# A weight clip that VectorE or GpSimd may take, ones columns on GpSimd, and new ranks for a planned schedule

## The chip, the cores and the metric

The kernel runs on one core of a Trainium2 chip. The metric is the device time of one execution in microseconds (us); lower is better. Three executions of the kernel before gave 1592.62, 1594.34 and 1591.09 us, median 1592.62. The engines are named as in the profile: PE (TensorE, matmul), PEld (its weight loads), DVE (VectorE), ACT (ScalarE), POOL (GpSimd), SP (SyncE, which here issues all DMAs).

## The reference

The input is q, k, v of 8 batches, 8 heads, 576 positions and 64 columns. First comes a linear attention, then two MLPs on its output of 4608 tokens by 512 columns:

```python
q_s = softmax(q, over the 64 columns);  k_s = softmax(k, over the 576 positions)
x = q_s @ (k_s^T @ v)                    # per batch and head
x = max(x @ w_in, 0)**2 @ w_out          # 512 -> 2048 -> 512
out = (sigmoid(x @ w_gate) * (x @ w_val)) @ w_out2   # 512 -> 1536 -> 512
```

The four MLP weights reach the kernel as 64-bit floats, seen as pairs of 32-bit words; q, k and v as 32-bit floats.

## The kernel before, in words

**Matmuls.** Tokens are taken in 9 blocks `j` of 512. Every float32 operand is split into a rounded part and the rest (`hi_of` on ACT, line 330; `lo_of` on DVE, line 333), and a product is three matmuls of 128x128 weights on 512 columns (`mm3`, lines 336 to 338). Blocks 0 and 1 and a part of block 2 go through the first layer with plain products, and block 0 through the second as well, up to about 216 us. From then on products run in a seven-product scheme over pairs of blocks (`plan_seven`), with sums of weights and of activations made by DVE.

**Weights.** 68 pieces of 128x512 are read (16 of `w_in`, 16 of `w_out`, 24 of `w_gate` and `w_val`, 12 of `w_out2`) and each is made from 64-bit to 32-bit floats by seven steps that `plan_raw` (line 456) lists: `wl` loads; `wa` (ACT, line 381) takes the magnitude of the high word, `wc` (ACT, line 387) scales the low word; `wp` (`w_clip`, DVE, line 391) clips the magnitude between two constants; `wb` (DVE, line 397) shifts and masks; `wg` (DVE, line 404) puts the sign in; `wr` (DVE, line 411) adds the low word. Then come the split (`wh` on ACT, `wo` on DVE, at line 425 the sums of weights `wm`), a store to DRAM, and fetches for later blocks.

**Attention.** `plan_k` (line 797) does k and v of a batch. `v_ones` (`vo`, lines 561 to 569) copies a column of ones ahead of each head's columns: on POOL for batch 0 (line 569), on ACT for batches 1 to 7 (line 567). `plan_q` (line 829) does the softmax of q for a block and a pair of heads. From block 2 on a row's 64 columns lie on two groups of partitions, so maxima and sums are exchanged between the groups: `q_swap` (`qaw`, `qbw`, line 700) is four POOL copies of 32x32. DVE waits for the exchange in `q_sub` (line 710) and in `q_sum` (line 729).

**What sets the order.** Every step is given to `Plan.add` with a rank (`key`), the engines that may do it with a price in us, what it comes after, and the buffers that it takes and gives back. `Plan.trace` (line 173) plays these prices through before the program is built: whenever an engine is free by the prices, it takes the step of lowest rank that is ready. That play emits the instructions, so it fixes each engine's order; on the chip each engine works through its own list in order, and waits where something is late. A step with two engines in its price table goes to whichever asks first; the engines are asked in the order DMA, PE, ACT, DVE, POOL. `SHIFT` (line 31) is a table of offsets that `add` puts on the ranks, by kind of step and, for some, by index; it alters nothing but ranks. Lists named `worder`, `fetched`, `xorder`, `sorder` keep loads, fetches and splits in a fixed sequence. In all that, only PE, ACT, DVE and POOL lists and the single DMA list of SP are affected by the ranks.

```python
add(t + 0.2, {DVE: 0.35}, ("wp",) + key, w_clip, key, after=[("wa",) + key])
add(t + 0.25, {DVE: 0.35}, ("wb",) + key, w_bits, key, after=[("wp",) + key])
```

Of the kernel before, what the change touches and what calls it, by code (L numbers as in the profile page):

```python
# [16 lines left out]
AF = mybir.ActivationFunctionType  # L17
ALU = mybir.AluOpType
AX = mybir.AxisListType

E_MIN = 2.0**-15
E_MAX = 2.0**17 - 2.0**-7
# [31 lines left out]
    "chi": {(): 66.5, (0, 14): 22.9, (0,): 50.9},  # L54
    "clo": {(): 169.7, (0, 0): 68.2, (0, 1): 96.7, (0, 8): -2.6, (0,): 104.5},
# [6 lines left out]
    "kdg": {(): -380.9},  # L62
    "kgm": {(): -139.8, (3, 0): 59.1, (3,): 37.6},
    "km": {(): 7.9, (0,): -1830.8, (1, 0): -54.8, (1, 1): 52.3, (1, 1, 0): 61, (3, 1): 16.6, (5, 1, 2): 6.5, (6, 0): 5.7, (6, 0, 0): 2.1,
        (6, 0, 3): 41.2, (6,): 12.8, (7, 0): 9.8, (7, 0, 0): -13.4, (7,): 4},
    "kp": {(): -972.4},
    "ks": {(): -453.2},
    "kt": {(): -32.2, (0, 0): -38.4, (0, 1): -34.1, (0,): -35.9, (1, 0): -75.3, (2, 0): -66, (7, 0): 5.4, (7,): 5.8},
    "kt2": {(): 17, (1, 0): -59, (4, 0): -3.7, (4,): 12.2, (5,): 84.3, (6,): 13.3, (7,): -12.4},
    "ost": {(1, 2): 10.4, (1, 3, 1): -18.6, (1,): -14.6, (2, 0): 20.2, (2, 1, 1): 8.2, (2, 3): 19.2, (2, 3, 1): -16.7, (2,): -1.8, (3, 2): 6.1,  # L70
# [190 lines left out]
def attention_mlp_mlp(  # L261
# [127 lines left out]
    def w_clip(key):  # L389
        t = wf[key]  # L390
        nc.vector.tensor_scalar(out=t, in0=t, scalar1=E_MIN, scalar2=E_MAX, op0=ALU.max, op1=ALU.min)
# [1289 lines left out]
```

## Time and profile before

| what | value |
|---|---|
| median of three executions | 1592.62 us |
| the profiled execution's own time | 1590.78 us |
| its span in the profile | 1589.0 us |
| PE busy | 1555.6 us, 98% |
| DVE busy | 1199.8 us, 76% |
| ACT busy | 941.3 us, 59% |
| POOL busy | 48.4 us, 3% |
| granted PE clock, whole span | 0.998 of full speed |

The profiled execution's own time is 1.8 us over its span and 1.8 us under the median of the three. Busy times are of the whole span; the stretches differ greatly, so the rows below go by stretch. A matmul's record runs on after the next has begun, so a small gap between two matmuls doesn't show as PE idle.

### The profile page before, as it was taken

The page shows a single profiled execution, that of the slowest core. Times are in us where ns is not written, and L with a number is a line of the kernel's source. Part 1 is how long each engine was busy: PE and PEld are TensorE (multiplying, and loading weights), DVE is VectorE, ACT ScalarE, POOL GpSimd, SP SyncE. Part 2 cuts the span into 40 slices and gives each one's busy share as a digit, 9 for nine tenths or more (in the row PEclk, how much of TensorE's full clock was granted, in tenths as well). Part 3 has the DMA queues.
Part 4 walks back from the last instruction along what each step waited for, and adds up shares of the span by engine and source line. Part 5 has one row for each costly group of instructions (what it writes and reads, how often), then busy time and mean ns, then how long its engine had stood idle before and what let it go on. Part 6 is the DMA issues. An engine that isn't in the chain of part 4 may idle for free.

```text
span 1589.0 us, 22941 instructions
## 1 busy us (share of the span) xinstructions
PE 1555.6 (98%) x7892; PEld 1280.7 (81%) x7892; DVE 1199.8 (76%) x2069; ACT 941.3 (59%) x1730; POOL 48.4 (3%) x122
## 2 busy tenths in 40 slices
PE   5899999999999999999999999999999999999998
PEld 3678878787888778888888888888888888888898
DVE  8999997899999999885957895348733682358446
ACT  7978765787686858675845563336433552345344
POOL 0011000010100020000000000000000000000000
PEclk9999999999999999999999999999999999999999
DMA  8896899999999889999897999657865667555996
GB/s 311 316 324 223 328 359 346 345 346 352 353 341 345 308 306 323 338 342 335 300 370 230 340 346 301 215 190 262 254 222 197 226 225 237 189 198 188 268 399 232
DMA packets 205619, 462.02 MB, mean 291 GB/s; under 512 B 78784, under 2 KB 78784, under 8 KB 205504
## 3 DMA queue, kind: packets, MB, share of 16 engines
q1 hardware_dynamic: 205504, 460.56, 83.3%
q8 instruction: 63, 1.03, 0.3%
q14 instruction: 52, 0.43, 0.1%
HBM read 364.54 MB, written 95.94 MB: 290 GB/s over the span
## 4 chain that ended last, share of the span: by engine, by line
PE 81%; DVE 11%; DMA 3%; ACT 2%; issue 2%; POOL 1%; SPq 0%; DVEq 0%; ACTq 0%; POOLq 0%
PE bank L336 27%; PE bank L338 26%; PE bank L337 26%; DVE whl L333 1%; DMA qt<-in_q_dram 1%; DVE qst L688 1%; POOL qsw L700 1%; PE kps L622 1%; DVE wf L404 1%; DVE wf L411 1%; DVE qt L711 1%; PE xps L771 1%; DVE g0hl L333 1%; DVE bS L333 1%; DVE wf L425 1%
## 5 line engine op out<-in xcount | busy, mean ns | idle before, releaser
L336 PE MATMUL bank<-bX,ws 128*128 128x512 f32 (+1 forms) x1176 | 441.6, 376 | 1.1 <-ACT bank L330 0.8
L338 PE MATMUL bank<-bX,ws 128*128 128x512 f32 (+1 forms) x1176 | 439.8, 374 | 0.0
L337 PE MATMUL bank<-bX,ws 128*128 128x512 f32 (+1 forms) x1176 | 439.8, 374 | 0.0
L336 PE MATMUL bank<-bS,ws 128*128 128x512 f32 (+1 forms) x868 | 331.4, 382 | 2.3 <-ACT x L330 1.4
L337 PE MATMUL bank<-bS,ws 128*128 128x512 f32 (+1 forms) x868 | 329.2, 379 | 0.0
L338 PE MATMUL bank<-bS,ws 128*128 128x512 f32 (+1 forms) x868 | 328.9, 379 | 0.0
L965 DVE TENSOR_TENSOR s<-s,bank 128x512 f32<-128x512 f32 (+1 forms) x171 | 108.8, 647 | 211.2 <-PE bank L338 180.7
L330 ACT ACTIVATE bS<-s 128x512 fp32r<-128x512 f32 (+1 forms) x330 | 192.8, 600 | 117.9 <-PE bank L338 89.8
L336 PEld LDWEIGHTS bank<-bX,ws 128*128 128x128 f32 x1176 | 221.5, 188 | 42.4 <-DVE s L963 1.2
L338 PEld LDWEIGHTS bank<-bX,ws 128*128 128x128 f32 x1176 | 221.5, 188 | 39.4
L337 PEld LDWEIGHTS bank<-bX,ws 128*128 128x128 f32 x1176 | 221.5, 188 | 39.1
L333 DVE TENSOR_TENSOR bS<-s,bS 128x512 fp32r<-128x512 f32 (+1 forms) x330 | 210.6, 653 | 35.5 <-ACT bS L330 35.1
L330 ACT ACTIVATE s<-bank 128x512 f32<-128x512 f32 (+1 forms) x227 | 128.6, 573 | 144.3 <-PE bank L338 142.6
L336 PEld LDWEIGHTS bank<-bS,ws 128*128 128x128 f32 x868 | 163.3, 188 | 36.2 <-issue 1.9
L338 PEld LDWEIGHTS bank<-bS,ws 128*128 128x128 f32 x868 | 163.3, 188 | 30.7
L337 PEld LDWEIGHTS bank<-bS,ws 128*128 128x128 f32 x868 | 163.4, 188 | 30.3 <-DVE bS L333 0.4
L892 DVE TENSOR_TENSOR s<-s,s 128x512 f32<-128x512 f32 (+1 forms) x192 | 120.4, 653 | 0.8
L330 ACT ACTIVATE bank<-bank 128x512 f32<-128x512 f32 (+1 forms) x108 | 59.1, 556 | 90.9 <-PE bank L338 82.0
L330 ACT ACTIVATE whl<-wf 128x512 fp32r<-128x512 f32 x127 | 78.7, 626 | 42.3 <-PE bank L338 14.7
L983 ACT ACTIVATE s<-s 128x512 f32<-128x512 f32 (+1 forms) x60 | 35.3, 588 | 91.7 <-DVE s L965 91.7
L333 DVE TENSOR_TENSOR whl<-wf,whl 128x512 fp32r<-128x512 f32 x127 | 86.1, 685 | 2.9 <-ACT whl L330 2.2
L700 POOL COPY qsw<-qst 32x32 f32<-32x32 f32 x112 | 45.9, 410 | 527.1 <-DVE qst L688 502.9
(116 smaller groups left out, 1846.3 us busy)
## 6 DMA issues: line engine op xcount, KB each, us to landing
ws<-w_out SPq DMA_DIRECT2D x217, 512.0 KB, 5.2
ws<-w_gv SPq DMA_DIRECT2D x210, 512.0 KB, 4.5
ws<-w_in SPq DMA_DIRECT2D x100, 512.0 KB, 6.2
w_out<-whl SPq DMA_DIRECT2D x49, 512.0 KB, 4.1
w_gv<-whl SPq DMA_DIRECT2D x42, 512.0 KB, 6.2
w_in<-whl SPq DMA_DIRECT2D x32, 512.0 KB, 5.8
kt<-in_k_dram SPq DMA_DIRECT2D x16, 640.0 KB, 5.7
x2r<-x SPq DMA_DIRECT2D x36, 256.0 KB, 5.1
```

Of the source, the lines that this page charges most:

```text
L330: nc.scalar.activation(out=dst, in_=src, func=AF.Copy)
L333: by_name[engine].tensor_tensor(out=dst, in0=src, in1=hi.bitcast(F32), op=ALU.subtract)
L336: nc.tensor.matmul(ps, ah, bh, start=first, stop=False, skip_group_check=True)
L337: nc.tensor.matmul(ps, ah, bl, start=False, stop=False, skip_group_check=True)
L338: nc.tensor.matmul(ps, al, bh, start=False, stop=last, skip_group_check=True)
L404: nc.vector.scalar_tensor_tensor(out=w, in0=high, scalar=-0x40000000, in1=w, op0=ALU.bitwise_and, op1=ALU.bitwise_or)
L411: by_name[engine].tensor_tensor(out=w, in0=w, in1=low, op=ALU.add)
L425: by_name[engine].tensor_tensor(out=t[0], in0=t[1], in1=t[2], op=op)
L700: nc.gpsimd.tensor_copy(out=other[32 * a:32 * a + 32], in_=st.rearrange("p g o -> p (g o)")[32 * b:32 * b + 32])
L892: by_name[engine].tensor_tensor(out=t[o], in0=t[a], in1=t[b], op=ALU.subtract)
L965: nc.vector.tensor_tensor(out=t, in0=t, in1=src, op=ALU.add)
L983: nc.scalar.activation(out=t, in_=t, func=AF.Sigmoid)
```

## The change

The clip `wp` may be done by POOL (priced 0.8) or by DVE (0.35); the columns of ones `vo` of all batches go to POOL, priced 0.35 in place of ACT's 0.22; the prices of the two exchanges go from 0.8 to 1.45; and the whole `SHIFT` table is another one, with more entries and wider values. All other prices, buffers and steps stay.

```diff
 SHIFT = {
-    "bcb": {(('G', 'c', 0, 0),): 22.1, (('G', 'c', 0, 2),): 199.4, (('G', 'c', 1, 0), 'T2'): 3.7, (('G', 0, 0, 0), 'T1'): -2.2,
...
-    "kdg": {(): -380.9},
...
-    "x": {(): -1764.4, (4, 2): 52.3},
+    "bcb": {(('G', 'c', 0, 2),): 180.67, (('G', 0, 0, 0),): -121.1, (('G', 0, 0, 2), 'T4'): -21.27, (('G', 0, 0, 2),): -8.01,
...
+    "kdg": {(): -1270.4},
...
+    "x": {(): -2931.32, (4, 2): 184.42, (6, 2): 54.47},
...
-    def w_clip(key):
+    def w_clip(key, engine):
         t = wf[key]
-        nc.vector.tensor_scalar(out=t, in0=t, scalar1=E_MIN, scalar2=E_MAX, op0=ALU.max, op1=ALU.min)
+        by_name[engine].tensor_scalar(out=t, in0=t, scalar1=E_MIN, scalar2=E_MAX, op0=ALU.max, op1=ALU.min)
...
-            add(t + 0.2, {DVE: 0.35}, ("wp",) + key, w_clip, key, after=[("wa",) + key])
+            add(t + 0.2, {POOL: 0.8, DVE: 0.35}, ("wp",) + key, w_clip, key, CHOSEN, after=[("wa",) + key])
...
-        if b:
-            nc.scalar.activation(out=pad[:, :, 1:2], in_=row[:, :, 2 * D:2 * D + 1], func=AF.Copy)
-        else:
-            nc.gpsimd.tensor_copy(out=pad[:, :, 1:2], in_=row[:, :, 2 * D:2 * D + 1])
+        nc.gpsimd.tensor_copy(out=pad[:, :, 1:2], in_=row[:, :, 2 * D:2 * D + 1])
...
-            add(key + 2.5 * step, {ACT: 0.22}, ("vo",) + x, v_ones, *x, after=[("kt",) + n if b else ("vt",) + x])
+            add(key + 2.5 * step, {POOL: 0.35}, ("vo",) + x, v_ones, *x, after=[("kt",) + n if b else ("vt",) + x])
...
-            add(key + 0.3 * step, {POOL: 0.8}, ("qaw",) + n, q_swap, j, p, after=[("qa",) + n], take=["qw"])
+            add(key + 0.3 * step, {POOL: 1.45}, ("qaw",) + n, q_swap, j, p, after=[("qa",) + n], take=["qw"])
...
-            add(key + 2.3 * step, {POOL: 0.8}, ("qbw",) + n, q_swap, j, p, after=[("qb",) + n], take=["qw"])
+            add(key + 2.3 * step, {POOL: 1.45}, ("qbw",) + n, q_swap, j, p, after=[("qb",) + n], take=["qw"])
```

## Rows read from the trace of the kernel before

**Rows 1.** The stretches of the span: length, busy time of each engine, clock, DMA.

```profile
core 0: us, PE busy (x) PEld busy (x) DVE busy (x) ACT busy (x) POOL busy (x), PEclk, DMA share, GB/s
0.00:40.00 40.00, 22.39 (x154) 14.29 (x155) 34.45 (x66) 30.12 (x77) 2.49 (x10) 0.91 0.87 309
40.00:80.00 40.00, 34.78 (x239) 24.74 (x240) 37.92 (x73) 37.48 (x70) 0.00 (x0) 1.00 0.90 319
80.00:120.00 40.00, 38.15 (x257) 29.18 (x256) 36.35 (x65) 30.51 (x56) 7.76 (x24) 1.00 0.96 324
120.00:200.00 80.00, 80.00 (x400) 65.44 (x400) 78.03 (x136) 61.10 (x107) 8.46 (x25) 1.00 0.76 276
200.00:240.00 40.00, 37.48 (x163) 30.03 (x162) 36.99 (x63) 27.72 (x50) 0.00 (x0) 1.00 0.93 351
240.00:600.00 360.00, 358.88 (x1995) 287.38 (x1994) 335.26 (x572) 261.24 (x485) 29.67 (x64) 1.00 0.94 338
600.00:1589.00 989.00, 983.90 (x4693) 829.60 (x4691) 640.81 (x1100) 493.12 (x890) 0.00 (x0) 1.00 0.79 269
```

**Rows 2.** PE in order of time: start, duration, what; idle before it and releaser.

```profile
30.00 0.50 PE L336 MATMUL bank<-x,whl 128*128 128x512 f32 x1 [1.07 <-ACT x L330]
...
216.31 0.50 PE L336 MATMUL bank<-bS,ws 128*128 128x512 f32 x1 [1.41 <-ACT x L330]
...
218.18 0.50 PE L336 MATMUL bank<-bS,ws 128*128 128x512 f32 x1 [0.90 <-DVE x L1092]
```

**Rows 3.** The chain that ended last, 200 to 220 us: start, us, what.

```profile
200.11 0.34 DVE wf L391
...
203.32 0.35 DVE wf L391
...
217.52 0.61 DVE x L1092
218.13 0.04 issue
218.18 0.50 PE bank L336
```

**Rows 4.** The clips of line 391 by stretch: length, DVE busy (count), clock, DMA.

```profile
0.00:40.00 40.00, 2.10 (x5) 0.91 0.87 309
40.00:120.00 80.00, 5.98 (x15) 1.00 0.93 322
120.00:217.00 97.00, 4.90 (x12) 1.00 0.79 291
```

**Rows 5.** Groups of instructions on POOL: busy us, mean ns, idle before.

```profile
L700 POOL COPY qsw<-qst 32x32 f32<-32x32 f32 x112 | 45.9, 410 | 527.1 <-DVE qst L688 502.9 <-DVE kri L630 15.9 <-DVE qst L710 4.2
L569 POOL COPY vt<-vt 128x5 f32<-128x5 f32 x4 | 1.8, 463 | 10.5 <-DMA vt<-in_v_dram 10.5
masks.py:199 POOL TENSOR_SCALAR_AFFINE_SELECT ident<-ident 128x128 f32<-128x128 f32 x1 | 0.3, 292 | 0.1
```

**Rows 6.** POOL in order of time.

```profile
10.88 0.19 POOL L569 COPY vt<-vt 128x5 f32<-128x5 f32 x1 [9.58 <-DMA vt<-in_v_dram]
86.75 0.93 POOL L700 COPY qsw<-qst 32x32 f32<-32x32 f32 x4 [73.19 <-DVE qst L688]
561.60 5.21 POOL L700 COPY qsw<-qst 32x32 f32<-32x32 f32 x4 [14.17 <-DVE qst L688]
```

**Rows 7.** DVE in order of time beside that last exchange.

```profile
564.12 0.69 DVE L333 TENSOR_TENSOR bS<-p,bS 128x512 fp32r<-128x512 f32 x1
564.72 0.69 DVE L411 CUSTOM_DVE_ANT_0 wf<-wraw,wf 128x1024 uint16<-128x1024 uint16 x1
565.32 0.69 DVE L333 TENSOR_TENSOR bS<-p,bS 128x512 fp32r<-128x512 f32 x1
566.84 0.19 DVE L710 TENSOR_TENSOR qst<-qst,qsw 128x32 f32<-128x32 f32 x1 [0.83 <-POOL qsw L700]
```

**Rows 8.** Who waited for the exchanges: us in total, times, longest us.

```profile
DVE qst L710 <- POOL qsw L700: 3.4, 5, 0.8
DVE qst L729 <- POOL qsw L700: 3.4, 5, 0.8
```

**Rows 9.** The ones of line 567 by stretch: length, ACT busy (count), clock, DMA.

```profile
0.00:40.00 40.00, 0.31 (x2) 0.91 0.87 309
40.00:120.00 80.00, 0.92 (x6) 1.00 0.93 322
120.00:217.00 97.00, 0.70 (x4) 1.00 0.79 291
```

More of the change, by code (lines that the diff above doesn't have):

```diff
@@ L31 @@
 SHIFT = {
[22 rows of a table removed]
-    "chi": {(): 66.5, (0, 14): 22.9, (0,): 50.9},
-    "clo": {(): 169.7, (0, 0): 68.2, (0, 1): 96.7, (0, 8): -2.6, (0,): 104.5},
[6 rows of a table removed]
-    "kdg": {(): -380.9},
[L63 to L68, printed above, removed]
@@ L69 @@
-    "kt2": {(): 17, (1, 0): -59, (4, 0): -3.7, (4,): 12.2, (5,): 84.3, (6,): 13.3, (7,): -12.4},
-    "ost": {(1, 2): 10.4, (1, 3, 1): -18.6, (1,): -14.6, (2, 0): 20.2, (2, 1, 1): 8.2, (2, 3): 19.2, (2, 3, 1): -16.7, (2,): -1.8, (3, 2): 6.1,
[25 rows of a table removed]
-        ('out', 2, 2): 137.9, ('out', 2, 3): -149.4, ('out', 3): 89.3, ('out',): 45.2, ('out2', 1, 2): -24.1, ('out2', 2, 2): 22.5, (): 151.6},
[9 rows of a table removed]
-        ('out', 0, 0): 53.8, ('out', 0, 2): 51.1, ('out', 1, 1): 51.8, ('out2', 0): 40.3, (): 100.8},
[8 rows of a table removed]
-        ('out', 0, 'S4'): -33.9, ('out', 2): -65.1, ('out',): 96.9, (): 18.5},
[19 rows of a table removed]
[43 rows of a table added]
@@ new lines @@
+    "chi": {(): 3.71, (0, 12): 7.02, (0,): 53.98},
+    "clo": {(): 471.13, (0, 0): 264.69, (0, 1): 252.23, (0,): 409.28},
[7 rows of a table added]
+    "kdg": {(): -1270.4},
+    "kgm": {(): -899},
+    "km": {(): -21.94, (0,): -3197.62, (1,): 179.2, (5, 0, 0): -170.86, (5, 0, 2): 19.14, (5,): 32.04, (6, 1): -33.99, (6, 1, 2): -31.67,
+        (6, 1, 3): -35.07, (6,): 4.07, (7,): -34.37},
+    "kp": {(): -1463.85},
+    "kr": {(): 154.16, (6, 1): -165.66, (6,): -34.79, (7, 0): -127.02, (7, 1): -190.16},
+    "ks": {(): -1599.48},
@@ new lines @@
+    "kt": {(): -105.72, (0, 0): 53.12, (0, 1): 54.99, (0,): -146.43, (3, 1): 10.54, (5, 0): -5.58, (5, 1): -28.28, (5,): -9.82, (6, 0): -43.56,
+        (7, 0): 3.27, (7, 1): -24.77},
+    "kt2": {(): 21.69, (1, 1): 222.61, (4, 0): -86.63, (5, 0): -61.14, (5,): 78.64, (6, 0): -23.55, (6, 1): -24.1, (7,): -12.87},
+    "ost": {(): -13.3, (0,): -53.34, (1, 0): -65.18, (1, 0, 0): -44.46, (1, 1): -61.21, (1, 2): -55.1, (1, 2, 0): 131.94, (1, 3, 1): -112.12,
[18 rows of a table added]
+        ('out', 1): -266.74, ('out', 1, 1): -168.29, ('out', 1, 2): -73.67, ('out', 1, 3): -70.86, ('out', 2): -385.76, ('out', 2, 0): -10.82,
+        ('out', 2, 3): -313.06, ('out', 3): -93.35, ('out',): 90.34, ('out2', 0, 0): -9.25, (): 680.79},
[4 rows of a table added]
+        ('in',): 269.94, ('out', 0): 25.98, ('out', 1): -233.29, ('out', 1, 3): -87.44, ('out',): 146.19, ('out2', 2): -21.27, ('out2', 2, 2): -98.53,
+        (): 173.94},
@@ new lines @@
+    "wc": {('gv', 1, 3): -32.27, ('gv', 3): -42.2, ('gv', 4, 0): 32.32, ('gv', 4, 1): -166.53, ('gv', 4, 3): -165.23, ('gv', 5, 0): -142.99,
+        ('in',): 2663.43, ('out', 0): 49.57, ('out', 0, 2): -67.87, ('out', 1, 1): -136.8, ('out', 2): -385.57, ('out', 2, 3): -295.23,
+        ('out',): 14.89, (): 743.55},
[33 rows of a table added]
+        ('in', 2, 3): 40.69, ('out', 0, 1): -93.29, ('out', 0, 2): -53.83, ('out', 1): -166.73, ('out', 2): -318.93, ('out', 3): -43.47,
[16 rows of a table added]
+        ('out', 3, 3): -210, (): 108.56},
[4 rows of a table added]
+        ('in', 3, 1): -149.83, ('in',): -20.09, ('out', 0): -19.43, ('out', 0, 3): -142.5, ('out', 0, 7): -90.34, ('out', 1): -132.45,
+        ('out', 2): -49.7, ('out', 2, 3): -34.56, ('out', 3): -85.29, ('out', 3, 3): -82.99, ('out', 3, 4): -90.87, ('out', 3, 5): -121.43,
[9 rows of a table added]
```

219 rows, old and new, of the table SHIFT are left out of this document.

## The prediction

> **What bounds the kernel now.** I read the stretches first [rows 1]. The PE clock is at its upper level, 2.4 GHz, in every stretch but the first 40 us, so the clock has nothing to give. What counts is PE's idle time, length minus busy: 17.6 us in 0 to 40, 5.2 in 40 to 80, 1.9 in 80 to 120, none in 120 to 200, 2.5 in 200 to 240, 1.1 in 240 to 600, and 5.1 from 600 to the end. The change alters no matmul, so only this idle time can be won. The last 5.1 us are the results' way out after the last matmul. The first 17.6 us come almost all before the first large matmul at 30.00 us [rows 2], while k and q are loaded and go through the softmax. That leaves 5.2 + 1.9 + 2.5 + 1.1 = 10.7 us within reach, nearly all of it before 240 us.
>
> Who holds PE up there? DVE is busy 37.92 of 40 us and ACT 37.48 of 40 in the stretch 40 to 80, and DVE 78.03 of 80 in 120 to 200 [rows 1]. The chain of waits runs through DVE up to 218 us, the clips of line 391 among its pieces, and it passes to PE's matmuls at 218.18, where PE had sat idle for 0.90 us on a DVE copy, after 1.41 us on an ACT split a little before [rows 2, 3]. After that PE has its matmuls fed: DVE still has 335 of 360 us of work up to 600, yet PE idles only 1.1 us. So DVE's load up to 217 us is the thing to watch, and what the change does to DVE later is worth at most that 1.1 us.
>
> **The change part by part.**
>
> The clip. Of the 68 clips 5 + 15 + 12 = 32 lie before 217 us [rows 4]; 27 of them after 40 us. On the chain one clip occupies 0.34 to 0.35 us of DVE [rows 3]. The plan asks DVE first, but a DVE that is busy over nine tenths of the time is rarely free at the moment when a clip becomes ready, so nearly all 27 should go to POOL. Taken off: 27 x 0.35 = 9.5 us of DVE.
>
> What it costs on POOL, no row shows for this shape. The nearest rows are the columns copy of 128x5 in 0.19 us [rows 6] and the select of 128x128 in 0.292 us [rows 5]: (0.292 - 0.19) / 123 columns is 0.83 ns a column, and 512 columns would take 0.19 + 507 x 0.00083 = 0.61 us, an estimate. 27 of these are 16.5 us, and POOL is busy only 16.2 us between 80 and 200 [rows 1]: POOL has room. The clip is one link of a chain on one piece (magnitude, clip, shift, sign, add), so 0.61 in place of 0.35 us delays only that piece, which the plan fetches ahead.
>
> What it pays back is DVE waiting for POOL. The exchange shows how POOL fares beside a busy DVE. Undisturbed, four copies take 0.93 us; beside a row of back-to-back DVE instructions they took 5.21 us, and DVE's own instructions of 128x512 kept their 0.60 us pace and 0.69 us length meanwhile [rows 6, 7]. So DVE isn't slowed by POOL's small copies; it pays where it needs the result: 0.83 us of idle time at 566.84 [rows 7]. Over the 28 exchanges (112 copies of four each [rows 5]) that happened 10 times and cost 3.4 + 3.4 = 6.8 us [rows 8], 0.24 us an exchange. The clip's cost to DVE lies between nothing (it fits behind other DVE work) and that 0.83 us each time. I take the mean of the exchange, the nearest row with the same pair of engines: 27 x 0.24 = 6.5 us. Net relief of DVE: 9.5 - 6.5 = 3.0 us. Ends: 9.5 us won, or 27 x (0.83 - 0.35) = 13 us lost.
>
> Here a page speaks against the change. Between POOL and DVE the rows show POOL waiting and DVE not. The Trainium skill, "SBUF — State Buffer", section "Who interferes with whom", says that the two share one pair of ports as an exclusive lock: a POOL instruction that starts first keeps it for its whole length, and a DVE instruction with two SBUF inputs is fully blocked until then. No row here has a POOL instruction long enough to show it; by that rule the clip would be no relief but a loss, and it stands among the rivals.
>
> The price of the exchanges. Nothing new runs; DVE's waiting step is placed 0.65 us later, so that other ready work goes in front of it. 12 of the 28 exchanges lie before 200 us (24 + 25 copies, by the counts in [rows 1]), and 12 x 0.24 = 2.9 us of DVE waiting is the most to win. I take half, 1.5 us; at the other end nothing.
>
> The columns of ones. 28 ACT copies become POOL copies. Before 217 us these are 2 + 6 + 4 = 12, with 0.31 + 0.92 + 0.70 = 1.9 us of ACT [rows 9]. ACT is the fuller engine only between 40 and 80 us; I take 0.5 us of PE time, between 0 and 1.9. On POOL such a copy takes 0.19 us by itself and 0.463 on average [rows 5, 6], and it is now queued with clips and exchanges; k's matmuls wait for it, four steps later in the chain, so I cost it at nothing. If it came behind a starved clip it could cost its k block what the longest exchange lost, 4.3 us.
>
> The ranks. They change the order on every engine and on SP's list of DMAs, not the work. They could win the rest of the 10.7 us, or undo some of the stretch after 600 us where PE now runs without a gap. Nothing in the trace says which; I take 0. No list gets a DMA more or less.
>
> **The sum.** 3.0 + 1.5 + 0.5 = 5.0 us off the span of 1589.0, thus 1584.0, and 1585.8 for the profiled execution's own 1590.78. The median of the runs is 1.8 us above that execution, so the forecast is 1587.6 us, 0.3% faster. Its own range goes from the whole 10.7 us won (1581.9) to the bound of what can be told from no change, 0.2% or about 3.2 us (1589.4).
>
> **The rivals.**
>
> *No measurable change*, 1592.6, within 3.2 us: what DVE wins comes out in 120 to 200 us, where PE is busy 40 of 40 anyway, or is paid back in waits of just 0.35 us a clip, the point where gain and loss meet. For it: PE's busy share is 98% and most of the DVE-heavy stretch shows no PE idle at all. Against it: the chain ran through DVE up to 218 us. That most clips stay on DVE, since DVE is asked first, also ends here.
>
> *DVE waits for POOL* (slower): the plan sets the shift step 0.95 us after the clip begins, but beside back-to-back DVE work POOL gets no turn until DVE stops at that very step, as at 566.84. If that decides 60% of the 27 clips at 0.83 us and the rest cost nothing, DVE loses 16 x 0.83 - 27 x 0.35 = 3.8 us; if it decides nearly all, 13. I take 8: 1600.4 us. It decides from a mean wait of 0.35 us a clip. For it: one third of the exchanges ended in such a wait. Against it: the mean was 0.24.
>
> *POOL holds DVE up* (slower): a running clip makes the next DVE instruction stand for the estimated 0.61 us. 27 x (0.61 - 0.35) = 7.0 us, 1599.6 us. Against it: no DVE instruction beside the exchanges is longer than its fellows [rows 7]. For it: those copies have 32 columns. This is what the page's rule above makes of it.
>
> *Faster by more than the sum*: the new order also brings forward the first large matmul, out of the 17.6 us of the first stretch. Three us more would be 1579.
>
> **How the numbers follow.** Forecast and the better end: 0.50 faster. No measurable change: 0.24. Slower: 0.14 for DVE waiting and 0.12 for POOL holding, 0.26 together. The range goes down to 1579, the best case, and up to 1603, past both slower rivals and short of the 13 us bound (1605.6), which leaves out some 1 in 10.
>
> **What would show it.** Right: line 391 appears on POOL over 50 times at about 0.6 us or more, DVE's busy time falls by some 20 us over the span, PE idle between 40 and 240 us falls from 9.6 to about 5 us, and after 600 us PE has its 5.1 us of idle time and no more. Wrong on the clip: waits of DVE's line 397 on POOL of over 9.5 us before 217 us (the first slower rival), or DVE instructions of 128x512 lasting 1.2 us and more beside POOL clips (the second). Wrong on the ranks: PE idle times on DMA or ACT where there were none, above all after 240 us, or a first large matmul well away from 30 us.

## The result: 1.2% slower, and the profile after

The changed kernel takes 1611.38 us (median of four runs, 1609.54 to 1615.25) against 1592.62: a ratio of 1.0121, interval 1.0098 to 1.0143. Its profiled execution took 1609.54 us with a span of 1607.7, so 18.7 us more than the span before. The line numbers have moved: 391 of before, the clip, is 446; 397, the shift, is 452; 404, the sign, is 459; the matmuls of lines 336 to 338 are now 391 to 393, and the splits of 330 and 333 are 385 and 388.

Here are the stretches of the changed kernel, as in [rows 1].

```profile
core 0: us, PE busy (x) PEld busy (x) DVE busy (x) ACT busy (x) POOL busy (x), PEclk, DMA share, GB/s
0.00:40.00 40.00, 21.49 (x142) 14.20 (x143) 31.56 (x57) 28.23 (x71) 15.93 (x18) 0.87 0.79 292
40.00:80.00 40.00, 33.23 (x229) 23.55 (x228) 36.33 (x62) 35.62 (x64) 15.33 (x9) 0.96 0.87 306
80.00:120.00 40.00, 37.27 (x207) 28.59 (x206) 34.22 (x58) 27.75 (x48) 13.62 (x24) 1.00 0.87 298
120.00:200.00 80.00, 77.59 (x422) 61.55 (x421) 71.56 (x119) 57.12 (x100) 35.59 (x45) 0.98 0.74 263
200.00:240.00 40.00, 38.44 (x165) 30.25 (x164) 36.76 (x61) 26.52 (x47) 7.08 (x3) 1.00 0.88 312
240.00:600.00 360.00, 357.27 (x1977) 286.42 (x1976) 328.07 (x551) 260.45 (x470) 80.07 (x86) 1.00 0.95 341
600.00:1607.70 1007.70, 999.68 (x4761) 839.09 (x4759) 653.51 (x1110) 505.22 (x909) 23.32 (x20) 1.00 0.81 268
```

DVE is *less* busy than before in every stretch up to 600 us (71.56 of 80 against 78.03 in 120 to 200), and yet PE stands idle more: 18.5 + 6.8 + 2.7 + 2.4 + 1.6 + 2.7 + 8.0 = 42.7 us against 33.4. Idle time is only half of the loss, though: for the same 7892 matmuls PE's busy time grew as well, from 1555.6 to 1565.0 us; the last section comes back to that. A less busy DVE on the path that feeds PE doesn't mean relief; here it means that DVE itself waits. The groups on POOL, as in [rows 5], and the waits for them, as in [rows 8], say for what:

```profile
L446 POOL TENSOR_SCALAR wf<-wf 128x512 f32<-128x512 f32 x54 | 119.4, 2216 | 425.0 <-ACT wf L436 406.3 <-DMA w_in<-whl 8.3 <-DVE qst L740 5.6
L752 POOL COPY qsw<-qst 32x32 f32<-32x32 f32 x112 | 45.5, 406 | 134.7 <-DVE qst L740 129.3 <-DVE qst L781 1.3 <-DVE kri L682 0.4
L621 POOL COPY vt<-vt 128x5 f32<-128x5 f32 x32 | 25.5, 827 | 166.9 <-DMA vt<-in_v_dram 101.8 <-PE bank L393 64.9
```

```profile
DVE wf L452 <- POOL wf L446: 25.8, 23, 2.5
```

54 of the 68 clips went to POOL, and there a clip takes long. The view of line 446 gives the shortest and the median in ns, on POOL and on DVE:

```profile
L446 POOL TENSOR_SCALAR wf<-wf x54: 1914/1956/5270, 16.5 to 916.1; 128x512 f32<-128x512 f32 x54
L446 DVE TENSOR_SCALAR wf<-wf x14: 420/427/431, 73.8 to 910.7; 128x512 f32<-128x512 f32 x14
```

At best 1.914 us, where the plan says 0.8, my estimate said 0.61, and DVE needs 0.42. So in 23 places DVE came to the shift of a piece before POOL had clipped it, and stood still for 25.8 us in all.

The second loss shows in DVE's own durations. This is DVE in order of time, and below it POOL:

```profile
56.80 0.68 DVE L466 CUSTOM_DVE_ANT_0 wf<-wraw,wf 128x1024 uint16<-128x1024 uint16 x1
57.40 1.10 DVE L459 SCALAR_TENSOR_TENSOR wf<-wraw,wf 128x512 int32<-128x512 int32 x1
58.42 0.41 DVE L631 TENSOR_TENSOR kmx<-kt 128x256 f32<-128x256 f32 x1
59.29 0.43 DVE L452 TENSOR_SCALAR wf<-wf 128x512 int32<-128x512 int32 x1 [0.46 <-POOL wf L446]
```

```profile
56.83 2.43 POOL L446 TENSOR_SCALAR wf<-wf 128x512 f32<-128x512 f32 x1 [4.53 <-ACT wf L436]
```

The clip begins at 56.83, and the sign step at 57.40 takes 1.10 us, where its median is 0.685; then the shift at 59.29 waits 0.46 us for the clip's end. Both losses meet in this one clip; over the span they do so in 8 clips. The sign step's shortest, median and longest durations, first before and then after:

```profile
L404 DVE SCALAR_TENSOR_TENSOR wf<-wraw,wf x68: 628/685/697, 18.2 to 898.5; 128x512 int32<-128x512 int32 x68
```

```profile
L459 DVE SCALAR_TENSOR_TENSOR wf<-wraw,wf x68: 629/685/1111, 18.9 to 922.2; 128x512 int32<-128x512 int32 x68
```

Counted over all DVE instructions: 33 last over 60 ns longer than the median of their form (same line, tiles and shape), the first at 19.82 us and the last at 916.23; every one overlaps a clip on POOL; none is over by more than 0.426 us; the sum is 11.8 us. In the kernel before there is none. So a clip holds DVE up, but mostly for some 0.41 us and not for its whole 1.92. "Held up" below always is this count (the expectations say 11.2 us, and 12.9 for c2, by a slightly different one).

### The profile page after: what moved, and what is told of

Read it like the earlier page. It is cut to its first block, busy times and chain, and to the rows that moved or that the text cites. A ratio compares the mean times of both kernels' runs of the same rounds, so it can differ in the third digit from the quotient of the medians.

```text
span 1607.7 us, 22980 instructions
## 1 busy us (share of the span) xinstructions
PE 1565.0 (97%) x7892; PEld 1283.6 (80%) x7892; DVE 1192.0 (74%) x2012; ACT 940.9 (59%) x1705; POOL 190.9 (12%) x204
## 4 chain that ended last, share of the span: by engine, by line
PE 69%; DVE 14%; DMA 4%; issue 4%; POOL 3%; ACT 3%; SPq 1%; DVEq 0%; POOLq 0%; ACTq 0%
PE bank L391 23%; PE bank L392 23%; PE bank L393 23%; POOL wf L446 3%; DVE bS L388 2%; DVE s L944 1%; DVE whl L388 1%; DVE wf L459 1%; DMA vt<-in_v_dram 1%; DVE wf L466 1%; DMA wraw<-in_moe_w_out_dram 1%; DVE qst L740 1%; SPq L424 1%; DVE bX L388 1%; POOL qsw L752 1%
## 5 line engine op out<-in xcount | busy, mean ns | idle before, releaser
L446 POOL TENSOR_SCALAR wf<-wf 128x512 f32<-128x512 f32 x54 | 119.4, 2216 | 425.0 <-ACT wf L436 406.3
```

The source lines that it names most:

```text
L446: by_name[engine].tensor_scalar(out=t, in0=t, scalar1=E_MIN, scalar2=E_MAX, op0=ALU.max, op1=ALU.min)
```

## The experiments

Two theories came first: **C**, the clip on POOL is the loss; **R**, the new ranks are. In the plan both hang together, since a price alters the order. So some runs keep the plan as it is and alter only which engine an instruction is issued on, in the same place of the order.

**Same order, clips back on DVE (a1)**

```diff
-        by_name[engine].tensor_scalar(out=t, in0=t, scalar1=E_MIN, scalar2=E_MAX, op0=ALU.max, op1=ALU.min)
+        nc.vector.tensor_scalar(out=t, in0=t, scalar1=E_MIN, scalar2=E_MAX, op0=ALU.max, op1=ALU.min)
```

> The changed kernel with every step in the same place and the same ranks, but the clips that it gave to POOL are issued on DVE at that place of the order. Theory C (the clip on POOL is the loss: 1.92 us where 0.8 was planned, DVE waiting 25.8 us for it and held up for 11.2 us): back to about the kernel before, 1587 to 1597 us, although DVE gets some 19 us of clips more. Theory R (the new ranks are the loss): stays at 1604 us or more.

1597.62 us, ratio to before 1.0024 (1.0014 to 1.0034), 0.6 us above the range of theory C. Although DVE has 54 clips more to do, 13.8 of the 18.8 us are gone by the medians (some 11 to 19 by the two intervals). Theory C holds for these. What is left, 4.7 us over the kernel before (2.2 to 5.4 by the interval), is not the clip on POOL.

**The kernel before, same order, clips on POOL (d1)**

```diff
-        nc.vector.tensor_scalar(out=t, in0=t, scalar1=E_MIN, scalar2=E_MAX, op0=ALU.max, op1=ALU.min)
+        nc.gpsimd.tensor_scalar(out=t, in0=t, scalar1=E_MIN, scalar2=E_MAX, op0=ALU.max, op1=ALU.min)
```

> The kernel before, same ranks, prices and order, with all 68 clips issued on POOL. Theory C: in this order the shift step stands close behind the clip, so DVE waits for POOL on most pieces, over 1 us each, and the time is well above the change's, 1612 to 1660 us. Theory R: 1590 to 1600 us.

1633.66 us, 1.0252 (1.0237 to 1.0267): 40.3 us lost with the old ranks untouched, with all 68 clips on POOL. In this order the shift stands close behind the clip, and the wait grows:

```profile
DVE wf L397 <- POOL wf L391: 65.0, 45, 5.6
```

**Is it the clip's length? (b4)** The clip with its lower bound alone:

```diff
-... scalar1=E_MIN, scalar2=E_MAX, op0=ALU.max, op1=ALU.min)
+... scalar1=E_MIN, scalar2=None, op0=ALU.max)
```

> The changed kernel with the clip cut to its lower bound (one operation in place of two; the upper bound is left out). If POOL's time is spent on the operations, the clip falls from 1.92 to 1.0 to 1.4 us while it still reads 512 columns and holds DVE for about 0.41 us. Theory L (the length of the clip in its chain is the loss): 1598 to 1606 us. Theory H (holding up DVE is the loss): 1608 to 1613 us, as the change. If the clip stays at 1.9 us this tells nothing between them.

```profile
L446 POOL TENSOR_SCALAR wf<-wf x54: 1482/1614/4829, 17.3 to 910.1; 128x512 f32<-128x512 f32 x54
```

```profile
DVE wf L452 <- POOL wf L446: 17.3, 18, 1.8
```

The operations were not most of the clip's time: it fell to 1.48 us at best, not to 1.0 to 1.4. That was enough: DVE's waiting fell by 8.5 us, it was held up much as before (11.4 us), and the time fell by 6.6 us to 1604.76 (1.0070, 1.0055 to 1.0085). The length counts through DVE's waits.

**Is it the holding up? (c2, e2)** Clips on DVE; wherever POOL had a clip, two instructions of 256 columns that nobody waits for:

```diff
+    spare_o = cst.tile([128, 256], mybir.dt.uint8, name="spare_o")
...
-        by_name[engine].tensor_scalar(out=t, in0=t, scalar1=E_MIN, scalar2=E_MAX, op0=ALU.max, op1=ALU.min)
+        nc.vector.tensor_scalar(out=t, in0=t, scalar1=E_MIN, scalar2=E_MAX, op0=ALU.max, op1=ALU.min)
+        if engine == POOL:
+            for _ in range(2):
+                nc.gpsimd.tensor_scalar(
+                    out=spare_o.rearrange("p (o c) -> p o c", c=128), in0=ident.rearrange("p (o c) -> p o c", o=1).to_broadcast([128, 2, 128]),
+                    scalar1=E_MIN, scalar2=E_MAX, op0=ALU.max, op1=ALU.min,
+                )
```

> As a1 (the changed kernel's order, clips on DVE), but wherever the change gave a clip to POOL, POOL does two instructions of 256 columns on a constant tile that nobody waits for. They hold DVE for some 0.2 us each and keep POOL busy, but are no link of a weight's chain. Theory H: 1604 to 1612 us. Theory L: 1596 to 1601 us, as a1. In between, the parts can be read off: a1 is 1597.6.

```profile
L450 POOL TENSOR_SCALAR spare_o<-ident x108: 1052/1116/4866, 13.8 to 631.4; 128x256 uint8<-128x256 f32 x108
```

1610.02 us, 1.0104 (1.0089 to 1.0119), 12.4 us above the same kernel without them (a1). No piece of weight waits for them; DVE is held up for 13.5 us (74 instructions, at most 0.23 us each). But k's matmuls need ones that now stand behind such an instruction in POOL's list, so it was run again with the ones of batches 1 to 7 on ACT:

```diff
-        nc.gpsimd.tensor_copy(out=pad[:, :, 1:2], in_=row[:, :, 2 * D:2 * D + 1])
+        if b:
+            nc.scalar.activation(out=pad[:, :, 1:2], in_=row[:, :, 2 * D:2 * D + 1], func=AF.Copy)
+        else:
+            nc.gpsimd.tensor_copy(out=pad[:, :, 1:2], in_=row[:, :, 2 * D:2 * D + 1])
```

> As c2 (clips on DVE, two idle POOL instructions of 256 columns where the change had a clip), with the ones of batches 1 to 7 on ACT, so that nothing but the exchanges stands behind them. Theory H (holding up DVE, 12.9 us in c2): 1606 to 1611 us, near c2's 1610. Theory Q (c2 lost its 12.4 us to the ones behind the idle instructions): 1598 to 1602 us.

1607.34 us, 1.0083 (1.0068 to 1.0098), with 13.1 us of holding up. The same kernel without the idle work is c3 below, 1598.52 us, so the loss is still 8.8 us. POOL work that nobody needs thus costs 8.8 to 12.4 us for some 13 us of holding up; some 3 us may be due to what stands behind it, but the intervals of the two runs overlap.

**The ones (e1, c3, d2).** The same edit in the changed kernel, clips on POOL, then in the kernel with clips on DVE; and the reverse, all ones on POOL, in the kernel before at the same order:

> The changed kernel, clips on POOL, with the columns of ones of batches 1 to 7 issued on ACT at the same place of the order. Theory Q (part of the loss is k's matmuls waiting for ones that stand behind clips in POOL's list, 6.7 us of waits of the weight loads on line 446): 1602 to 1607 us. Theory D (the loss is DVE's time alone: 25.8 us waiting, 11.2 us held up): 1608 to 1613 us.

> As a1, with the columns of ones of batches 1 to 7 issued on ACT at the same place of the order. Theory O (the remaining 4.7 us over before come from ones on POOL, that take 1.16 us on average there): 1590 to 1594 us. Theory R (they come from the ranks): 1596 to 1600 us.

> The kernel before, same ranks, prices and order, with the ones of batches 1 to 7 issued on POOL. All theories: within 3 us of before, 1590 to 1596 us, since no POOL work of any length stands in front of them.

1612.77 us (1.0114, 1.0097 to 1.0132) beside the change's 1.0121; 1598.52 us (1.0027, 1.0014 to 1.0039) beside 1.0024; 1593.47 us (0.9996, 0.9987 to 1.0005) beside before. All three show no difference: where the ones of batches 1 to 7 are made is worth nothing that can be told. I had laid 6.7 us at their door: waits of PE's weight loads that the profile puts down to a clip on POOL. 2.3 of them went without effect. The other one, 4.4 us (4.7 in the first of these runs), is no wait for ones. It stands before the first batch's matmuls, whose ones were ready at 13.17 us. In the changed kernel these rows lead up to the matmuls:

```profile
12.97 0.20 POOL L621 COPY vt<-vt 128x5 f32<-128x5 f32 x1 [0.23 <-DMA vt<-in_v_dram]
21.44 0.43 DVE L452 TENSOR_SCALAR wf<-wf 128x512 int32<-128x512 int32 x1 [0.80 <-POOL wf L446]
21.78 1.48 DVE L658 TENSOR_TENSOR kt<-kt,bank 128x1280 f32<-128x1280 f32 x1
23.29 1.27 ACT L662 ACTIVATE kt<-kt 128x1280 f32<-128x1280 f32 x1 [0.81 <-DVE kt L658]
24.66 2.43 PE L674 MATMUL bank<-vt,kt 128*64 128x65 f32 x40 [4.14 <-POOL wf L446]
```

PE began 0.1 us after ACT's exponential of k (line 662), which had waited for DVE's subtraction (line 658), and that stood behind a shift that waited for a clip. So the clip reaches PE here through DVE's list, not through the ones. PE's wait is not all new: in the kernel before it idles 3.06 us ahead of the same matmuls.

**The prices and the ranks (a3, a4, b2, c4).** The changed kernel with the clip on POOL priced at what it takes:

```diff
-            add(t + 0.2, {POOL: 0.8, DVE: 0.35}, ("wp",) + key, w_clip, key, CHOSEN, after=[("wa",) + key])
+            add(t + 0.2, {POOL: 1.95, DVE: 0.35}, ("wp",) + key, w_clip, key, CHOSEN, after=[("wa",) + key])
```

> The changed kernel with the clip on POOL priced at 1.95 us in the plan, all else the same. Theory C by its part that the plan was wrong on the length: the waits of DVE's line 452 on POOL fall from 25.8 us to under 10, the time to 1596 to 1604 us; DVE is still held up by about 0.4 us a clip. Theory R: about 1608 to 1614 us, since the ranks are the same.

```profile
DVE wf L452 <- POOL wf L446: 3.3, 5, 1.9
40.00:80.00 40.00, 29.66 (x209) 20.58 (x210) 32.26 (x57) 31.43 (x56) 10.90 (x7) 0.96 0.88 314
```

1608.44 us, 1.0100 (1.0079 to 1.0120). The waits went, as expected, and the time hardly moved: theory C's range failed, and the time lies in the one given for theory R. PE's idle time in 40 to 80 us is now 10.3 us (29.66 busy) where the change has 6.8. A new price made a new order (48 clips on POOL in place of 54), with ranks that were not made for it. That this order is what it lost to is argued, not shown. How much a price can do by itself, the next three show: the old ranks with all the new prices; the same with the clip on DVE alone; and the kernel before with nothing but the exchange at 1.45.

```diff
-            add(key + 0.3 * step, {POOL: 0.8}, ("qaw",) + n, q_swap, j, p, after=[("qa",) + n], take=["qw"])
+            add(key + 0.3 * step, {POOL: 1.45}, ("qaw",) + n, q_swap, j, p, after=[("qa",) + n], take=["qw"])
...
-            add(key + 2.3 * step, {POOL: 0.8}, ("qbw",) + n, q_swap, j, p, after=[("qb",) + n], take=["qw"])
+            add(key + 2.3 * step, {POOL: 1.45}, ("qbw",) + n, q_swap, j, p, after=[("qb",) + n], take=["qw"])
```

> The clip, the ones and the exchange prices as changed, with the ranks of the kernel before. Theory C: slower than before by about as much as the change or more, 1602 to 1618 us. Theory R: 1588 to 1597 us.

> The ranks of before, the clip on DVE alone; of the change only the ones on POOL and the longer exchange prices. Theories C and R both: within 5 us of before, 1588 to 1597 us. Theory O (columns of ones that queue behind other POOL work cost k's matmuls time): 1598 us or more.

> The kernel before with the price of the two exchanges at 1.45 in the plan and nothing else changed. Theory P (ranks fit only the prices that they were made for, so any new price upsets the order): 1600 to 1630 us, a good part of the 32 us that old ranks with the new prices of ones and exchanges lost. If a truer price helps by itself: 1585 to 1593 us.

1644.36 us (1.0319, 1.0302 to 1.0335), 1625.58 (1.0205, 1.0187 to 1.0223) and 1627.93 (1.0210, 1.0195 to 1.0225). The first lies above the range of either theory, the second above that of theories C and R both. The last is the kernel before with two numbers in the plan changed and the same instructions on every engine, and it loses 34 us. The first two differ in the plan by the clip alone, and by 18.8 us; but their orders differ too, so this is no price of the clip. I had blamed the ones for whatever the second would lose; the exchange's price alone loses as much. In the last one, DVE waits only 1.7 us for the exchanges, and new PE idle time has come: 11.6 us in 240 to 600, where the kernel before has 1.1, and 9.0 us in two stretches that hold no exchange at all and in which it has none. First the two stretches in the kernel before, then in this run:

```profile
760.00:800.00 40.00, 40.00 (x177) 32.91 (x177) 39.57 (x67) 33.05 (x60) 0.00 (x0) 1.00 0.86 300
800.00:840.00 40.00, 40.00 (x179) 33.11 (x178) 16.67 (x27) 14.84 (x24) 0.00 (x0) 1.00 0.97 369
```

```profile
760.00:800.00 40.00, 38.05 (x167) 30.84 (x165) 31.60 (x55) 31.66 (x58) 0.00 (x0) 1.00 0.97 312
800.00:840.00 40.00, 32.92 (x129) 26.06 (x130) 36.36 (x60) 22.92 (x41) 0.00 (x0) 0.87 0.84 292
```

The chain of that stretch has loads and fetches among its longest pieces:

```profile
769.76 4.26 DMA ws<-w_in
...
781.82 4.67 DMA wraw<-in_moe_w_out_dram
...
815.53 5.76 DMA w_out<-whl
```

**What the runs add up to.** Where the order is kept, the loss can be set against DVE's time: waits for the clip, plus holding up, minus 0.35 us for each clip that DVE no longer does.

| run, against the same order | waits | held up | taken off | DVE in sum | time |
|---|---|---|---|---|---|
| the change, against clips on DVE (a1) | 25.8 | 11.8 | 54 x 0.35 = 18.9 | +18.7 | +13.8 |
| clip of one operation (b4), against a1 | 17.3 | 11.4 | 18.9 | +9.8 | +7.1 |
| idle POOL work (c2), against a1 | 0 | 13.5 | 0 | +13.5 | +12.4 |
| the same with ones on ACT (e2), against c3 | 0 | 13.1 | 0 | +13.1 | +8.8 |
| before, clips on POOL (d1), against before | 65.0 | 12.5 | 68 x 0.35 = 23.8 | +53.7 | +40.3 |

Each us of DVE costs 0.67 to 0.92 us of the end. Where the order is another, the account doesn't hold: for a3 it would come to 3.3 + 8.7 - 48 x 0.35 = -4.8 us, and a3 is 10.8 us slower than a1. Of the change's 18.8 us, 13.8 are the clip on POOL. For the rest (4.7 us between a1 and the kernel before on the same chip) the ones are not the cause; ranks, exchange price and the clip's 0.8 in the plan are left, and these three were not told apart: with the clip on DVE alone in the plan, the new ranks lead the play into a dead end (no step that is left can get its buffers), so they were not timed by themselves. Nor is it known how a3 loses what its waits no longer cost. No run here beats the kernel before.

## Why the prediction was wrong

**What bounds the kernel** was read rightly in part: PE needs what DVE delivers, and DVE's time is worth 0.67 to 0.92 of its length. But a slower DVE costs PE after 240 us too: 4.5 of the 9.3 us of new idle time come there (2.7 against 1.1 us, and 8.0 against 5.1), where the text had put what the change does to DVE later at 1.1 us at most. And "the clock has nothing to give" didn't ask what it could take. **How many clips move** was right as well: 29 of 32 up to 230 us, 54 of 68 in all, "over 50" as written.

**The step that failed is the clip's price**: 0.61 us, from a slope between a five-column copy and a select of 128 columns [rows 5, 6]. It measured 1.914 at best. The two rows were of other operations, and the slope between them did not carry over to this one. With it fell "0.61 in place of 0.35 us delays only that piece": at 1.9 us the shift's place in the order comes too early.

**The wait per clip** was taken from the exchange, 0.24 us [rows 8]; it measured 25.8 / 54 = 0.48 us, above the 0.35 where gain and loss meet. The sign that the text had set for it, over 9.5 us before 217 us, came:

```profile
DVE wf L452 <- POOL wf L446: 12.2, 14, 1.8
```

An exchange of 0.93 us was no model for a job twice as long. **Holding up** was put at nothing in the sum, since no DVE instruction beside the exchanges was longer than its fellows [rows 7]; beside clips of 512 columns it is some 0.41 us at a time, in 33 of 54 clips. The small copies could not show it, as the text said, and still the sum took the side of those rows. In the sum's own terms, before 217 us: 29 x 0.35 = 10.2 us were taken off DVE, and 12.2 us of waits and 7.3 us of holding up were put on it, a loss of 9.3 us in place of the 3.0 won.

The Trainium skill, "SBUF — State Buffer", section "Who interferes with whom", has the engine that comes second blocked for the whole instruction of the first. The trace agrees that POOL holds DVE up, but not on the extent: in the changed kernel DVE is held for at most 0.426 us beside a clip of 1.914 us or more.

**The two slower rivals** were set against each other, and both came true. The waits, 25.8 us, are 6.9 us more than the 18.9 us of clips taken off DVE, near the 7.8 us of the first rival (its text says 8). Holding up, 11.8 us, is less than what was taken off and would have been no loss by itself: 0.22 us a clip, where the second rival had 0.61, and no DVE instruction of 128x512 reached the 1.2 us that was to be its sign. Together they are 18.7 us of DVE's time. The range ended at 1603 because it held the two to be alternatives and took the relief off in each. That the rivals' prices, 7.8 and 7.0 us, add up to nearly the 13.8 us that the clip cost is luck.

**The exchange's price** was to win 1.5 us, or nothing. DVE's waits for exchanges did fall when it was changed alone, from 6.8 to 1.7 us, and the kernel lost 34 us. The step "nothing new runs" overlooked that a price, like a rank, remakes every list. **The ranks** were put at 0; a1 shows +4.7 us for ranks and prices together, so the same term was unknown on both sides and belonged in the range at its full width. The first large matmul began at 31.61 us in place of 30.00, which was to be a sign of wrong ranks; but a1 has the same order and began it at 29.80, so here it was the clip. **The ones** at next to nothing were right. **DVE's busy time** was to fall by some 20 us and fell by 7.8, since the holding up gave 11.8 of the 18.9 back. **After 600 us** PE was to idle 5.1 us and idled 8.0. A slip that changes no number: the stretch 120 to 200 has PE busy for 80 of 80 us, not 40 of 40.

## What to carry to other kernels

Moving work from a full engine to an empty one is worth what the full engine gets back after its waits for the other and the time it is held up by it; take the price of the same operation and shape on the new engine from a measurement, not from the nearest other operation. Two ways in which a change can hurt, found side by side in a profile, may both come true: add them, and take the gain off once, before the range is closed. In a schedule that is played from prices, a price acts like a rank: test an engine or an instruction by issuing it at the same place of the old order, and only then let the plan move.

## What the runs showed of the hardware

In the runs at hand POOL took 1.914 us at best for a clip of 128x512 float32, 1.482 us with one of its two operations (b4), and 1.052 us for two operations on 256 columns with 8-bit output (c2). DVE instructions beside these ran longer by up to 0.426 us (0.448 in d1), 0.437 and 0.23 us. So POOL's time fell with one operation and DVE's holding up did not; with half the columns (and another output type) it was about half.

PE's clock took some more. These are matmuls of the changed kernel in order of time, from a gap of 2.27 us that an ACT step ended:

```profile
187.51 0.39 PE L393 MATMUL bank<-x,ws 128*128 128x512 f32 x1
190.16 0.50 PE L391 MATMUL bank<-x,ws 128*128 128x512 f32 x1 [2.27 <-ACT g L1116]
...
191.28 0.63 PE L391 MATMUL bank<-x,ws 128*128 128x512 f32 x1
191.71 0.63 PE L392 MATMUL bank<-x,ws 128*128 128x512 f32 x1
...
194.38 0.40 PE L393 MATMUL bank<-x,ws 128*128 128x512 f32 x1
194.61 0.39 PE L391 MATMUL bank<-x,ws 128*128 128x512 f32 x1
```

They follow each other every 0.23 us before, every 0.43 us from 190.85 to 193.84, and every 0.23 us again from 194.38 on. The granted clock was 0.50 from 190.58 to 193.99, the lower level, 1.2 GHz in place of 2.4. Seven of them at 0.2 us each are 1.4 us that stand in no idle time. In the kernel before, no stretch after 40 us has a mean granted clock under 1.00 [rows 1]; here 40 to 80 has 0.96 and 120 to 200 has 0.98. The same clock of 0.50 shows in 33.57 to 36.98 and in 43.81 to 47.22, where the kernel before has none. PE was busy throughout the three stretches, 10.2 us together, so by an estimate from the halved pace they cost some 5 of the 9.4 us by which PE's busy time grew; where the rest comes from is open.
